# Later head groups' weights asked for by ScalarE's DMA queue, and reordered by GpSimd one unit sooner, in an attention kernel with projections

## The chip, the cores and the metric

The kernel runs on one core of one Trainium2 chip. The metric is the device time of one execution in microseconds (us); a kernel is run several times, and its median is quoted with the lowest and highest run. A run also has a span, the time from the first to the last instruction in its trace.

## The reference

Eight batches of 112 query rows, 32 heads of size 192, 512 cached keys and values for each head. All tensors are bf16.

```python
B, Sq, D = 8, 112, 640
H, Sk, Dh = 32, 512, 192
q = (x @ wq).reshape(B, Sq, H, Dh).transpose(0, 2, 1, 3)
scores = einsum("bhqd,bhkd->bhqk", q, k_cache) * Dh ** -0.5
p = softmax(scores)
o = einsum("bhqk,bhkd->bhqd", p, v_cache)
return o.transpose(0, 2, 1, 3).reshape(B, Sq, H * Dh) @ wo
```

Nearly all bytes are K and V, 50 MB each. The two weight matrices have 7.9 MB each and are read once.

## The kernel before

The work is cut into 64 units of four heads and one batch (group `g` = heads 4g to 4g+3, eight batches in a group). In unit `u` TensorE makes the scores S(u), transposes an earlier output, makes the values PV(u-1), and fills the rest with query matmuls of a later group and output matmuls of an earlier one. ScalarE does the exponentials, VectorE transposes K, GpSimd copies three quarters of V into a denser layout ("middle copy", `vm`) and reorders the columns of the query weights (`wqr` to `wqs`). SyncE asks for all data through one DMA queue, in a list that is fixed when the program is built.

```python
def load_wq(g, dc):                       # group g, one of five 128-row blocks: 192 KB
    src = wq[128 * dc:128 * (dc + 1), 4 * DH * g:4 * DH * (g + 1)]
    ...
    add(wqr[:, dc, :], src, mWQ[dc], 16 * g, [(gW, DC * (g - 2) + dc + 1)])

def load_wo(g, k):                        # two requests of 160 KB, even and odd rows
    r0 = 4 * DH * g + 256 * k
    src = wo[r0:r0 + 256].rearrange("(p e) d -> p e d", e=2)
    for e in range(2):
        add(wos[:, g % 2, 2 * k + e, :], src[:, e], mWO[g % 2][k], 32 * (g // 2 + 1), [(pO, 2 * MT * (g - 1))])

for u in range(4, NU + 1):                # SyncE's list
    if u < NU: load_k(u)
    if u - 1 >= 3: load_v(u - 1)
    for g in range(2, NG):
        d = u - max(4, 8 * (g - 1) - 6)
        if 0 <= d < DC: load_wq(g, d)
    for g in range(1, NG):
        d = u - wo_round[g]
        if 0 <= d < 3: load_wo(g, d)
```

GpSimd's loop; the reorder of a block stands five units ahead of its group, at the start of the unit:

```python
at.setdefault(8 * (g - 1) - 5 + dc if g >= 2 else -1, []).append((g, dc))
...
for u in range(NU):
    for it in at.get(u, []):
        reorder(*it)
    W(gp, vRC, u + 1)
    ...                                   # three small range checks of the softmax sums
    if u + NM < NU:
        middle(u + NM)
```

TensorE's score block: 96 small matmuls on 32 rows each (`32*128` in the traces), each with its own weight load (6,144 of both in 64 units).

```python
def do_S(u):
    ...                                   # waits for kt, qT and for the exponentials of unit u-1
    for t in range(4):
        ...
        for c in range(6):
            for a in range(4):
                p = slice(32 * a, 32 * a + 32)
                mm = pe.matmul(ps[:, a, SQ * t:SQ * (t + 1)], kt[u % NT][p, t, c // 2, :, c % 2],
                               qT[g % 2][p, c, SQ * b:SQ * (b + 1)], start=(c == 0), stop=(c == 5))
```

## Time and profile before

| | before |
|---|---|
| time, median of the 3 runs at hand | 392.45 us (391.37 to 392.5) |
| profiled span | 389.5 us |
| TensorE busy | 384.3 us |
| share of the one data queue | 91.4% of the DMA engines' time |

TensorE is busy nearly all the time and carries the chain of waits; the prediction below shows those lines and reads them. Two further views of the kernel before matter for the end of the story. The prediction has the figures of the second, but not the first. The first is from the table of DMA queues (packets, MB, share of the 16 engines):

```profile
q8 instruction: 68, 1.11, 1.2%
```

This queue carries no data of the kernel. It brings the program: 68 packets and 1.11 MB, which is 16,384 bytes each. From the waits of SyncE (us in total, times, longest):

```profile
SPq L1334 <- DVE kt L1131: 34.8, 72, 1.6
SPq L1334 <- PE ps L992: 31.6, 25, 2.9
```

SyncE waits for 66 us until K buffers (freed by VectorE) and V buffers (freed by TensorE) are empty. It has time to spare once the early stage is over.

### The profile page before, as it was taken

How to read it: one execution, taken by the hardware profiler on the slowest of the kernel's cores; microseconds unless marked ns; L12 is line 12 of the kernel's file. 1: busy time of each engine (PE TensorE's matmuls, PEld its weight loads, DVE VectorE, ACT ScalarE, POOL GpSimd, SP SyncE). 2: the span in 40 equal slices, each digit the busy share in tenths (PEclk: the TensorE clock that was granted, in tenths of full speed). 3: DMA queues.
4: the chain of work that ended last, by engine and by line, in shares of the span. 5: the costliest groups of instructions: out<-in, count | busy, mean ns of one | idle time of the engine just before them, and what ended most of it. 6: DMA issues, size and time to landing. Idle time of an engine off the chain costs nothing.

```text
span 389.5 us, 19832 instructions
## 1 busy us (share of the span) xinstructions
PE 384.3 (99%) x8833; PEld 244.2 (63%) x8286; DVE 283.9 (73%) x506; ACT 249.8 (64%) x550; POOL 153.3 (39%) x352
## 2 busy tenths in 40 slices
PE   8999989999999999999999999999999999999997
PEld 4555665656666656756666575666656566676664
DVE  1665786676786888877677687777768777788934
ACT  3767764767657766666765866676585666656662
POOL 5442544343443353333453245324533322333231
PEclk9999999999999999999999999999999999999999
DMA  8999999999998999999999999799999989889712
GB/s 271 375 369 343 334 319 347 352 332 341 335 356 289 346 337 345 342 310 320 321 319 351 320 299 310 252 312 361 322 318 340 323 282 291 277 267 325 259 40 71
DMA packets 88584, 120.00 MB, mean 308 GB/s; under 512 B 9776, under 2 KB 88496, under 8 KB 88496
## 3 DMA queue, kind: packets, MB, share of 16 engines
q1 hardware_dynamic: 88496, 118.72, 91.4%
q8 instruction: 68, 1.11, 1.2%
q14 instruction: 20, 0.16, 0.1%
HBM read 117.54 MB, written 1.15 MB: 305 GB/s over the span
## 4 chain that ended last, share of the span: by engine, by line
PE 97%; issue 1%; POOL 1%; DVE 1%; DMA 0%; ACT 0%; SPq 0%
PE ps L953 22%; PE ps L878 22%; PE ps L992 22%; PE ps L974 21%; PE ps L1003 6%; PE ps L912 2%; PE ps L897 1%; PE ps L874 1%; DMA vs<-in_v_cache_dram 0%; POOL vm L1234 0%; PE ps L917 0%; POOL wqs L1227 0%; DVE kt L1131 0%; DVE acc L1151 0%; ACT oT L1089 0%
## 5 line engine op out<-in xcount | busy, mean ns | idle before, releaser
L1131 DVE STREAM_TRANSPOSE kt<-kr 128x384 int32<-128x384 int32 x256 | 195.0, 868 | 12.9 <-DMA kr<-in_k_cache_dram 11.6
L1072 ACT ACTIVATE pT<-ps 128x448 bf16<-128x448 f32 x256 | 131.3, 560 | 88.6 <-PE ps L974 87.1
L974 PEld LDWEIGHTS ps<-qT,kt 32*128 32x128 bf16 x6144 | 77.2, 93 | 30.1 <-issue 22.0
L953 PE MATMUL ps<-wos,oT 128*128 128x320 bf16 (+2 forms) x342 | 93.0, 299 | 0.0
L992 PE MATMUL ps<-vm,pT 128*128 128x193 bf16 x768 | 91.3, 247 | 0.8 <-ACT oT L1089 0.8
L878 PE MATMUL ps<-wos,oT 128*128 128x320 bf16 x330 | 91.2, 299 | 0.0
L974 PE MATMUL ps<-qT,kt 32*128 32x112 bf16 x6144 | 87.7, 208 | 0.4 <-DVE kt L1131 0.3
L1251 POOL TENSOR_SCALAR bad<-rinv 112x4 f32<-112x4 f32 x64 | 14.7, 229 | 183.7 <-DVE rinv L1137 183.5
L1234 POOL COPY vm<-vs 128x1152 int32<-128x1152 int32 x64 | 73.5, 1149 | 27.3 <-issue 20.7
L992 PEld LDWEIGHTS ps<-vm,pT 128*128 128x128 bf16 x768 | 68.5, 97 | 20.3 <-ACT oT L1089 9.6
L953 PE MATMUL ps<-xT,wqs 128*128 128x448 bf16 x210 | 74.0, 352 | 0.7 <-POOL wqs L1227 0.7
L878 PE MATMUL ps<-xT,wqs 128*128 128x448 bf16 x210 | 73.9, 352 | 0.0
L1079 ACT ACTIVATE os<-ps,rinv 112x192 bf16<-112x192 f32 x128 | 48.1, 440 | 25.3 <-DVE rinv L1137 25.3
L992 PE MATMUL ps<-vs,pT 128*128 128x193 bf16 x256 | 62.6, 245 | 0.0
L953 PEld LDWEIGHTS ps<-wos,oT 128*128 128x128 bf16 x342 | 33.2, 97 | 43.9 <-issue 37.2
L1056 ACT ACTIVATE qT<-ps 128x448 bf16<-128x448 f32 x96 | 47.8, 554 | 16.0 <-PE ps L953 11.2
L1154 DVE TENSOR_TENSOR acc<-ps,acc 128x320 f32<-128x320 f32 x84 | 37.4, 486 | 21.2 <-PE ps L953 21.0
L1089 ACT ACTIVATE oT<-ps 128x672 bf16<-128x672 bf16 x64 | 46.4, 725 | 1.3 <-PE ps L1003 1.3
L1137 DVE RECIPROCAL rinv<-ps 112x4 f32<-112x4 f32 x64 | 11.1, 173 | 45.3 <-PE ps L992 45.3
L953 PEld LDWEIGHTS ps<-xT,wqs 128*128 128x128 bf16 x210 | 20.3, 97 | 33.2 <-issue 26.6
L1140 DVE TENSOR_TENSOR os<-ps,rinv 112x384 bf16<-112x384 f32 x64 | 35.7, 558 | 7.0
L1227 POOL COPY wqs<-wqr 128x384 bf16<-128x384 bf16 x70 | 33.4, 509 | 4.9 <-DMA wqr<-in_wq_dram 4.9
(44 smaller groups left out, 155.9 us busy)
## 6 DMA issues: line engine op xcount, KB each, us to landing
kr<-in_k_cache_dram SPq DMA_DIRECT2D x256, 192.0 KB, 4.0
vs<-in_v_cache_dram SPq DMA_DIRECT2D x256, 192.0 KB, 4.0
wos<-in_wo_dram SPq DMA_DIRECT2D x48, 160.0 KB, 4.1
wqr<-in_wq_dram SPq DMA_DIRECT2D x35, 192.0 KB, 5.2
wqs<-in_wq_dram SPq DMA_DIRECT2D x5, 192.0 KB, 4.1
out_dram<-xs SPq DMA_DIRECT2D x6, 160.0 KB, 2.1
xs<-in_x_dram SPq DMA_DIRECT2D x2, 320.0 KB, 3.2
xs<-in_x_dram SPq DMA_DIRECT2D x1, 480.0 KB, 5.3
```

Of the source, the lines that this page charges most:

```text
L878: return pe.add_instruction(mybir.InstMatmult(name=nc.get_next_instruction_name(), engine=mybir.EngineType.PE, ins=[pe.lower_ap_or_imm(rhs ...
L953: mm = (pe.matmul if h == hs[0] and f == 0 else held)(ps[:, bank_of(pair, h), cs], w, rhs[h][:, cs], q == 0, q == n - 1 and f == cuts - 1)
L974: mm = pe.matmul(ps[:, a, SQ * t:SQ * (t + 1)], kt[u % NT][p, t, c // 2, :, c % 2], qT[g % 2][p, c, SQ * b:SQ * (b + 1)], start=(c == 0), ...
L992: mm = pe.matmul(pv[:, k, e, 0:DH + 1], pT[u % 2][:, a, t, :], src[:, a, v0:v0 + DH + 1], start=(t == 0), stop=(t == 3), skip_group_check= ...
L1056: act.activation(qT[g % 2][:, c, HQ * h:HQ * (h + 1)], ps[:, bank_of_Q0(n) if g == 0 else 6 + h, 0:HQ], ACTF.Copy).then_inc(aQ, 1)
L1072: act.activation(pT[u % 2][:, a, :, 0:SQ], ps[:, a, 0:4 * SQ].rearrange("p (t q) -> p t q", t=4), ACTF.Exp, scale=scale).then_inc(aEX, 1)
L1079: ins = act.activation(os_[u % 2][:, DH * (2 + e):DH * (3 + e)], pv_of(u)[0:SQ, 1, e, 0:DH], ACTF.Copy, scale=rinv[:, u % 4, 2 + e:3 + e])
L1089: act.activation(oT[:, :, SQ * b:SQ * (b + 1)].rearrange("p (k c) q -> p k c q", k=2), src.rearrange("p k (c q) -> p k c q", c=3), ACTF.Co ...
L1131: dve.transpose(dst, src).then_inc(vKT, 1)
L1140: dve.tensor_tensor(os_[u % 2][:, 0:2 * DH].rearrange("p (e d) -> p e d", e=2), pv[0:SQ, 0, :, 0:DH], rinv[:, u % 4, 0:2][:, :, None].broa ...
L1154: ins = dve.tensor_tensor(ob[:, m, cs] if g == NG - 1 else acc[:, m, cs], src, acc[:, m, cs], op=ALU.add)
L1234: gp.tensor_copy(vm[u % NM][:].rearrange("p a (t w) -> p a t w", w=RW)[:, :, :, 0:DH].bitcast(I32), vs[u % NV][:, :, 32:32 + 3 * DH].rearr ...
```

## The change

SyncE hands 72 weight requests to ScalarE (30 of `wq` for groups 2 to 7, 42 of `wo` for groups 1 to 7), so that K and V no longer stand behind them. They also stand earlier, three or four rounds by the loops' indices. GpSimd reorders one unit sooner, and no longer at the head of the unit but after the range checks and ahead of the middle copy.

```diff
+        def weight_loads(i):
+            got = []
+            for g in range(2, NG):
+                d = i - max(1, 8 * (g - 1) - 10)
+                if 0 <= d < DC:
+                    got.append((wqr[:, d, :], wq[128 * d:128 * (d + 1), 4 * DH * g:4 * DH * (g + 1)], mWQ[d],
+                                gW, DC * (g - 2) + d + 1))
+            for g in range(1, NG):
+                k = i - (wo_round[g] - 4)
+                if 0 <= k < 3:
                     ...                              # the two requests of load_wo
+            return got
@@ on_scalar, end of a unit @@
                 evac_pair(i, 1)
+                for dst, src, s, ws, wv in weight_loads(i):
+                    W(act, ws, wv)
+                    act.dma_start(dst, src).then_inc(s, 16)
@@ on_gpsimd @@
-                    at.setdefault(8 * (g - 1) - 5 + dc if g >= 2 else -1, []).append((g, dc))
+                    at.setdefault(8 * (g - 1) - 6 + dc if g >= 2 else -1, []).append((g, dc))
             for u in range(NU):
-                for it in at.get(u, []):
-                    reorder(*it)
                 W(gp, vRC, u + 1)
                 ...
+                for it in at.get(u, []):
+                    reorder(*it)
                 if u + NM < NU:
                     middle(u + NM)
@@ on_sync @@
-                for g in range(2, NG):  ...  load_wq(g, d)
-                for g in range(1, NG):  ...  load_wo(g, d)
```

## The prediction

> **What bounds the kernel now.** I read the page first: engine shares, then the chain of work that ended last, then the waits of TensorE.

> ```profile
> PE 384.3 (99%) x8833; PEld 244.2 (63%) x8286; DVE 283.9 (73%) x506; ACT 249.8 (64%) x550; POOL 153.3 (39%) x352
> ...
> q1 hardware_dynamic: 88496, 118.72, 91.4%
> ...
> PE 97%; issue 1%; POOL 1%; DVE 1%; DMA 0%; ACT 0%; SPq 0%
> ```

> The reader should see two limits close together. TensorE is busy in 384.3 of 389.5 us and carries 97% of the chain; the one DMA queue is busy 91% of the span. A busy matmul row need not mean a full one, so I checked the starts in the chain: 320-column output matmuls follow each other every 0.135 us, 448-column query matmuls every 0.19 us, 16 value matmuls take 1.35 us and 96 score matmuls 1.29 us, unit after unit. Those are the shortest spacings that the trace has for each shape, so inside a block nothing is to be gained. What remains is idle time between blocks, which the waits of TensorE and the longest pieces of the chain show:

> ```profile
> PE ps L992 <- ACT oT L1089: 0.8, 1, 0.8
> PE ps L953 <- POOL wqs L1227: 0.7, 1, 0.7
> PE ps L974 <- DVE kt L1131: 0.3, 1, 0.3
> ```

> After the start-up I find by spacing only about 2.6 us of lost TensorE time in the whole run: 1.0 at 57.4 us (values wait for ScalarE's oT copy), 0.86 at 65.95 us (the first query matmul of group 2 waits for GpSimd's reordered weights), and four score blocks with 0.08 to 0.17 us each. Only the 0.86 belongs to the change. It is a chain, read from the timeline of GpSimd:

> ```profile
> 60.11 0.20 POOL L1254 TENSOR_TENSOR cnt<-cnt,bad 112x8 f32<-112x8 f32 x1
> 63.85 1.15 POOL L1234 COPY vm<-vs 128x1152 int32<-128x1152 int32 x1 [3.53 <-issue]
> 64.94 0.96 POOL L1227 COPY wqs<-wqr 128x384 bf16<-128x384 bf16 x2
> ```

> GpSimd was free at 60.3 us, but the middle copy of unit 8 stood first in its order and waited 3.5 us for V of unit 8 (it landed at 63.74). The last reorder of group 2 came behind it, and ended at 65.9, just when TensorE wanted it.

> Last, the early stage. SyncE issues nearly back to back until about 60 us, and the stretches show a full DMA:

> ```profile
> 20.00:40.00 20.00, 20.00 (x499) 11.99 (x473) 12.76 (x21) 14.05 (x32) 6.49 (x13) 1.00 1.04 357
> 40.00:60.00 20.00, 18.89 (x431) 12.68 (x402) 15.65 (x29) 13.65 (x30) 10.59 (x23) 1.00 0.99 324
> ...
> 240.00:380.00 140.00, 140.00 (x3372) 91.14 (x3162) 105.90 (x190) 91.17 (x203) 51.48 (x114) 1.00 0.87 284
> ```

> The last two columns are the DMA share and GB/s. Up to about 80 us K and V land just in time: the V landing starts the middle copy of units 2 to 11. Later both land 3 us or more before their readers.

> [...]

> **The change part by part.**

> (a) SyncE loses 30 query and 42 output weight requests, 72 x 0.475 us (their pitch in the trace) = 34 us of issue. After 60 us SyncE waits for DVE (34.8 us) and for TensorE (31.6 us) anyway, so that is worth nothing later. Early, the issue was already slowed by a full DMA (single issues of 1.2 to 1.6 us in place of 0.43), so little there either. Gain: about 0.

> (b) ScalarE gains 72 x 0.475 = 34 us. They stand at the end of a unit, where ScalarE waits for the next scores (87.1 us over 64 units, mean 1.36). I set requests against the idle time before, unit by unit. One request needs 0.475 and the least idle time is 0.49; two need 0.95 against 1.07 or more, but 0.80 and 0.85 in two late units. Three need 1.42, in units 3, 4, 5, 30, 38 and 39, where the idle time is 0.49, 1.07, 1.85, 1.09, 1.09 and 1.85. The excess is 0.93+0.36+0.34+0.34+0.25 = 2.2 us in all. Of that the oT copy can pass on perhaps a third, as it has about 0.1 us of room before the value matmuls where a half pair stands between, but about 0.8 after a full pair: cost 0.7 us. If the sequencer runs ahead, nothing: the requests go out while ScalarE still computes. I take 0.2.

> (c) Reorder sooner and ahead of the middle copy: it now starts at about 60.3 and ends at 61.3 (2 x 0.48), 4.6 us ahead of need. The 0.86 goes. In the other 29 units the middle copy starts up to 0.96 us later: it ends about 3.2 us after the value block, and the fourth exponential wants it after about 3.9 at least; where V is late the reorder fits into the wait. Cost 0. Gain 0.86.

> (d) Weights asked for sooner. From the trace, old requests for wq of group 2 went out at 31.1, 35.4, 40.5, 46.5 and 53.5 us, for wo of group 1 at 47.9, 54.0 and 59.6. New ones, at ScalarE's unit ends: wq at 27, 33, 39.5, 44.5, 49.5; wo at 40, 45, 50; and wq of group 3 from 55.6 in place of 65.2. At 45 to 50 us that is 0.85 MB ahead of the old order, at 57 us about 0.5, at 63 about 0.4. At 350 GB/s, K and V are late by 2.4, 1.5 and 1.1 us. Room of V before TensorE must wait (exponential 4 to the next scores): unit 4 1.6 us, unit 5 2.3, unit 6 2.5, unit 7 1.3, unit 8 1.4. So about 0.2 us is lost. [...] Such losses don't add up unit by unit: each stall gives the DMA the same time to catch up. I take 0.6.

> Sum: -0.86 + 0.2 + 0.6 = about -0.1 us. From the median before, 392.45, which is at the upper edge of its three runs (mean 392.1), I say 391.9.

> **The rivals.**
> - Gain through a freed SyncE: K and V no longer queue behind weights, the early stage runs smoother, and the other early stalls (1.0 + 0.5) shrink too. For it: 20 to 60 us of nearly gapless issue. Against: the DMA share of 1.0 there, and the 1.0 us at 57.4 has an empty slot ahead of it and a chain of exponential and oT copy that no load touches. It would give 389.8 to 390.8.
> - Early V starved: the wait for weights is replaced by one for V, and so for the fourth exponential. For it: V's room of 1.3 to 2.5 us in units 4 to 8[...]. Against: all of these bytes are needed anyway and the lead is made once. It gives 392.5 to 394.
> - ScalarE as a new bound: a request that takes 1.0 us or more[...] would exceed the idle time in some 30 units, passing on 0.2 to 0.5 us each: 6 to 15 us, 398 to 407. For it: 1.2 to 1.6 us issues of SyncE. Against: the waits on semaphores are met long before (five units for the reorder), the ScalarE queue is nearly empty of requests[...].

> **Range and chances.** The middle cases span -1.5 to +1.5 us about 392, and runs before differ by 1.1 us, which gives 389.8 to 394.2. To be 2% faster, 7.8 us would have to go where only 2.6 us are lost: 0.01. Only the third rival makes it 2% slower: 0.04. Within 2%: 0.95.

> **What would show it.** (a) A second hardware queue with some 13 MB (30 x 197 KB + 42 x 164 KB); SyncE issues 531 loads and waits more. (b) ScalarE busy as before, and its wait for scores little changed; requests from its sequencer of about 0.45 us, before the unit's end if it runs ahead. (c) TensorE's wait for wqs gone, reorders ending before the middle copy of the same unit. (d) V of units 4 to 8 landing 1 to 4 us later against TensorE, waits of ScalarE for vm above the 1.5 us of before, score blocks waiting for pT before 65 us. Wrong would be: any ScalarE request above 1 us past 80 us with a value block behind it, or a span off by more than 3 us.

## The result, and the profile after

| | before | changed |
|---|---|---|
| time, median of 6 runs each | 391.91 us (390.65 to 392.92) | 397.76 us (395.76 to 400.23) |
| profiled span | 389.5 us | 396.8 us |
| ratio of fast runs | | 1.0155, 95% interval 1.0113 to 1.0197 |

A ratio is the mean time of one kernel's fast runs over that of the other's of the same rounds, so it is not quite the ratio of the medians. The change is within 2%, as predicted, but the time lies 3.6 us above the predicted range. The profiled pair lies a little further apart (7.3 us of span) than the medians of the six runs (5.9 us). Where did 7.3 us of span come from?

The page of the changed kernel first: engine shares, queues, the head of the chain of waits, and the weight requests (KB each, median us to landing).

```profile
PE 386.1 (97%) x8833; PEld 244.8 (62%) x8286; DVE 284.1 (72%) x506; ACT 249.8 (63%) x550; POOL 153.5 (39%) x352
...
q1 hardware_dynamic: 78128, 105.94, 79.4%
q10 hardware_dynamic: 10368, 12.78, 9.8%
q8 instruction: 68, 1.11, 1.1%
...
PE 97%; issue 2%; DVE 0%; ACT 0%
...
wos<-in_wo_dram ACTq DMA_DIRECT2D x42, 160.0 KB, 4.7
wqr<-in_wq_dram ACTq DMA_DIRECT2D x30, 192.0 KB, 5.1
```

The second data queue is there with the expected 12.78 MB. No engine has more work: ScalarE has the same 249.8 us. TensorE's share fell from 99 to 97%, and in the chain "issue" rose from 1 to 2%: time in which the engine waited for nothing that the profile shows. The waits of TensorE say the same (us in total, times, longest):

```profile
PE ps L990 <- issue: 4.3, 8, 1.2
PE ps L969 <- issue: 1.9, 1, 1.9
...
PE ps L1008 <- ACT oT L1105: 0.8, 1, 0.8
PE ps L990 <- DVE kt L1150: 0.3, 1, 0.3
```

The wait for `wqs` has gone, as predicted. In its place are nine stops that name nobody, in score blocks (L990) and query or output matmuls (L969). Two of them in TensorE's timeline (start, length, what, in brackets the idle time before):

```profile
55.13 0.87 PE L990 MATMUL ps<-qT,kt 32*128 32x112 bf16 x56 [0.26 <-DVE kt L1150]
57.17 0.67 PE L990 MATMUL ps<-qT,kt 32*128 32x112 bf16 x40 [1.18 <-issue]
...
158.58 0.31 PE L969 MATMUL ps<-wos,oT 128*128 128x320 bf16 x1 [1.88 <-issue]
```

A score block has 96 matmuls and its only waits stand at its head. Here it breaks after 56. Nothing in the program is waited for between matmul 56 and 57, and no operand is late there that the program waits for. The same view of the kernel before, one block later:

```profile
60.51 1.36 PE L974 MATMUL ps<-qT,kt 32*128 32x112 bf16 x96
```

There the block is whole. The longest pieces of the chain of the changed kernel show that its breaks in this stage come at a regular distance:

```profile
49.49 0.80 PE ps L990 x55
50.29 0.49 issue
50.79 0.70 PE ps L990 x41
...
55.13 0.87 PE ps L990 x56
56.00 1.18 issue
57.17 0.71 PE ps L990 x40
...
62.24 0.80 PE ps L990 x56
63.04 0.50 issue
63.55 0.67 PE ps L990 x40
```

| from 12 us on | before | changed |
|---|---|---|
| lost at page ends | 0.72 us in 4 stops | 8.93 us in 15 stops |
| lost elsewhere | 1.03 us (0.86 of it the wait for `wqs`) | 0.17 us |
| page ends passed under 1.6 us after the fetch | 4 of 66 | 23 of 66 |
| TensorE past the last page end, to the start of a fetch, mean | 1.94 us | 2.42 us |

The changed kernel loses 8.93 + 0.17 = 9.10 us, the kernel before 0.72 + 1.03 = 1.75, and the difference of 7.3 us is the whole difference of the spans. Both kernels also have the 1.0 us at 57 us for ScalarE's `oT` copy.

The last two rows show what a stop waits for. Four fetches from the records of that queue, in us:

```
kernel    TensorE passed     fetch              TensorE passes    from fetch's end
          the last page end                     this page end     to the page end
before    50.47              52.19 to 53.07     55.48             2.41
before    55.48              57.80 to 58.68     61.17             2.49
changed   50.79              54.65 to 55.74     57.17             1.43, stopped
changed   57.17              61.01 to 62.07     63.55             1.48, stopped
```

Each of 66 fetches pairs with one page end, in order. In both kernels the fetch of a page begins at the earliest 0.9 us before TensorE's first matmul past the previous page end, and usually after it; it takes about 1.0 us (median 1.01 and 0.99); and no page end is passed sooner than 1.2 us after the packet's end. A page of TensorE's program lasts 390 / 66 = 5.9 us. Before, that leaves 5.9 - 1.9 (to the start) - 1.0 (the fetch) = 3.0 us, and the stops ended 1.2 to 1.6 us after a packet. From these means I estimate that a fetch that starts 2 us later leaves 1.0 us, too little, so that TensorE stands still. In the changed kernel fetches of the same size start later (the limits of 60 KB and 2.5 us below were chosen after the fact). Of its 66, 42 had over 60 KB of the second queue's data start in the 2.5 us before them: these began 2.84 us after the page end and 20 came too late (under 1.6 us). The other 24 began after 1.68 us, and 3 came too late. At least 8.8 of the 8.9 us are lost at page ends whose fetch had data of the second queue just ahead.

The remaining parts went nearly as the prediction said, or better. Reorder and middle copy of GpSimd:

```profile
61.53 0.20 POOL L1271 TENSOR_TENSOR cnt<-cnt,bad 112x8 f32<-112x8 f32 x1
61.79 0.96 POOL L1246 COPY wqs<-wqr 128x384 bf16<-128x384 bf16 x2
62.69 1.16 POOL L1253 COPY vm<-vs 128x1152 int32<-128x1152 int32 x1
```

The reorder no longer stands behind a middle copy that waits for V. ScalarE's requests, with its own work beside them:

```profile
43.17 0.42 ACT L1095 ACTIVATE os<-ps,rinv 112x192 bf16<-112x192 f32 x1 [1.01 <-DVE rinv L1156]
43.18 0.34 ACTq L1136 DMA_DIRECT2D wqr<-in_wq_dram  x1
43.49 0.41 ACT L1095 ACTIVATE os<-ps,rinv 112x192 bf16<-112x192 f32 x1
43.55 0.94 ACTq L1136 DMA_DIRECT2D wos<-in_wo_dram  x2
44.98 0.54 ACT L1088 ACTIVATE pT<-ps 128x448 bf16<-128x448 f32 x1 [1.08 <-PE ps L990]
```

The first request went out at 43.18 us, ahead of the activation at 43.49 that stands before it in the program. Three requests end at 44.49, before the scores that ScalarE waits for anyway. They cost nothing here. And the early stage (columns: stretch, its length, busy time and count of TensorE, weight loads, VectorE, ScalarE and GpSimd, then clock, DMA share and GB/s):

```profile
20.00:40.00 20.00, 20.00 (x502) 12.17 (x469) 13.31 (x21) 14.42 (x32) 7.15 (x15) 1.00 1.07 371
40.00:60.00 20.00, 17.22 (x411) 11.60 (x387) 14.34 (x26) 12.19 (x28) 9.39 (x19) 1.00 1.07 372
```

From 40 to 60 us the DMA moves 372 GB/s where it moved 324. K and V came hardly later for the weights put ahead: V of unit 6 landed at 51.19 us (50.48 before), V of unit 7 already at 56.75 (57.27 before). But TensorE, busy 18.89 us of this stretch before, has 17.22 now. The data that came sooner bought nothing. SyncE simply waits more for empty buffers:

```profile
SPq L1345 <- PE ps L1008: 68.8, 38, 4.6
SPq L1345 <- DVE kt L1150: 55.9, 89, 4.4
```

### The profile page after: what moved, and what is told of

Read it like the earlier page. It is cut to its first block, busy times and chain, and to the rows that moved or that the text cites. A ratio compares the mean times of both kernels' runs of the same rounds, so it can differ in the third digit from the quotient of the medians.

```text
span 396.8 us, 19856 instructions
## 1 busy us (share of the span) xinstructions
PE 386.1 (97%) x8833; PEld 244.8 (62%) x8286; DVE 284.1 (72%) x506; ACT 249.8 (63%) x550; POOL 153.5 (39%) x352
## 2 busy tenths in 40 slices
DMA packets 88585, 120.01 MB, mean 302 GB/s; under 512 B 9776, under 2 KB 88496, under 8 KB 88496
## 3 DMA queue, kind: packets, MB, share of 16 engines
q10 hardware_dynamic: 10368, 12.78, 9.8%
HBM read 117.54 MB, written 1.15 MB: 299 GB/s over the span
## 4 chain that ended last, share of the span: by engine, by line
PE 97%; issue 2%; DVE 0%; ACT 0%
PE ps L969 22%; PE ps L894 22%; PE ps L1008 21%; PE ps L990 21%; PE ps L1019 6%; PE ps L928 2%; PE ps L913 1%; PE ps L890 1%; PE ps L933 0%; DVE kt L1150 0%; ACT oT L1105 0%; DVE acc L1170 0%; PE ps L1025 0%; ACT pT L1088 0%; DVE xs L1173 0%
## 5 line engine op out<-in xcount | busy, mean ns | idle before, releaser
L990 PEld LDWEIGHTS ps<-qT,kt 32*128 32x128 bf16 x6144 | 77.6, 93 | 35.7 <-issue 27.7
L969 PE MATMUL ps<-wos,oT 128*128 128x320 bf16 (+2 forms) x342 | 93.1, 299 | 1.9 <-issue 1.9
L990 PE MATMUL ps<-qT,kt 32*128 32x112 bf16 x6144 | 89.3, 208 | 4.7 <-issue 4.3
L969 PE MATMUL ps<-xT,wqs 128*128 128x448 bf16 x210 | 74.0, 352 | 0.0
L969 PEld LDWEIGHTS ps<-wos,oT 128*128 128x128 bf16 x342 | 33.2, 97 | 46.0 <-issue 39.3
L969 PEld LDWEIGHTS ps<-xT,wqs 128*128 128x128 bf16 x210 | 20.3, 97 | 32.4 <-issue 26.8
```

Source lines behind the costliest of these rows:

```text
L969: mm = (pe.matmul if h == hs[0] and f == 0 else held)(ps[:, bank_of(pair, h), cs], w, rhs[h][:, cs], q == 0, q == n - 1 and f == cuts - 1)
```

## The experiments

The theory to test: (F) TensorE's program comes late because a second queue of data is active, so that the fetches of instructions begin later. Rivals: (R) GpSimd's new order does it; (A) ScalarE as issuer does it; (C) the weights are asked for too early and crowd out K, V or the fetches, on whatever queue; (N) the number of small requests does it. All time ratios are against the kernel before in the same rounds.

### 1. The reorder alone

The weights go back to SyncE's list; only GpSimd's two edits stay.

```diff
@@ against the changed kernel @@
-        def weight_loads(i): ...
-                for dst, src, s, ws, wv in weight_loads(i):
-                    W(act, ws, wv)
-                    act.dma_start(dst, src).then_inc(s, 16)
@@ on_sync @@
+                for g in range(2, NG):
+                    d = u - max(4, 8 * (g - 1) - 6)
+                    if 0 <= d < DC:
+                        load_wq(g, d)
+                for g in range(1, NG):  ...  load_wo(g, d)
```

> Only the reorder moves (one unit sooner, ahead of the middle copy); all weights stay on SyncE's queue. Theory A (the second hardware queue makes TensorE's instruction fetches late, which stops TensorE at every 256th instruction): no such stop above 0.3 us, the 0.86 us wait for wqs gone, ratio 0.996 to 1.000 (390.4 to 392 us). Rival B (the reorder ahead of the middle copy holds up the exponentials): ratio 1.008 or more. Rival C (weights asked for sooner crowd out K and V): ratio as under A, as nothing is asked for sooner.

Measured: 392.70 us median (391.53 to 395.36), ratio 0.9995 (0.9957 to 1.0033). The waits of TensorE in the profiled run, which was the slowest of the six:

```profile
PE ps L974 <- issue: 1.1, 2, 0.7
...
PE ps L992 <- ACT oT L1089: 0.8, 1, 0.8
...
PE ps L953 <- issue: 0.3, 1, 0.3
```

The wait for `wqs` is gone and three stops at page ends have 1.91 us (0.53, 0.94 and 0.44), so I missed with "no stop above 0.3": one queue alone can now and then be late too. GpSimd shows why the order matters, and not only the unit:

```profile
61.80 0.95 POOL L1227 COPY wqs<-wqr 128x384 bf16<-128x384 bf16 x2
64.09 1.15 POOL L1234 COPY vm<-vs 128x1152 int32<-128x1152 int32 x1 [1.34 <-DMA vs<-in_v_cache_dram]
```

The middle copy still waits for V, but with the reorder already done. The gain of 0.86 us does not come out of the scatter of the time. (R) falls.

### 2. The second queue alone

The reverse: GpSimd's loop as before, weights on ScalarE's queue.

```diff
@@ against the changed kernel, on_gpsimd @@
-                    at.setdefault(8 * (g - 1) - 6 + dc if g >= 2 else -1, []).append((g, dc))
+                    at.setdefault(8 * (g - 1) - 5 + dc if g >= 2 else -1, []).append((g, dc))
             for u in range(NU):
+                for it in at.get(u, []):
+                    reorder(*it)
                 W(gp, vRC, u + 1)
```

> Only the requests move to ScalarE's queue at their new times; the reorder stands where it stood before. Theory A: the loss stays whole, ratio 1.013 to 1.022, with 10 or more stops of TensorE at instructions that are 193 modulo 256 in its order and 6 us or more lost in them. Rival B: ratio below 1.004. Rival C: loss stays, but as waits on K or V before 80 us, not at these instructions.

Measured: 398.79 us (395.22 to 400.52), ratio 1.0137 (1.0088 to 1.0186), and 10.70 us lost in 15 stops at page ends.

```profile
PE ps L990 <- issue: 5.7, 9, 1.5
PE ps L969 <- issue: 1.9, 2, 1.6
```

The whole loss is in the queue.

### 3 and 4. Only `wq`, or only `wo`, on ScalarE's queue

Number 3 keeps the 30 `wq` requests on ScalarE (5.9 MB), number 4 the 42 of `wo` (6.9 MB); the other half goes back to SyncE's list at its old places.

```diff
@@ number 3, weight_loads @@
-            for g in range(1, NG):
-                k = i - (wo_round[g] - 4)
-                ...
@@ number 3, on_sync @@
+                for g in range(1, NG):  ...  load_wo(g, d)
@@ number 4, weight_loads @@
-            for g in range(2, NG):
-                d = i - max(1, 8 * (g - 1) - 10)
-                ...
@@ number 4, on_sync @@
+                for g in range(2, NG):  ...  load_wq(g, d)
```

> Only the 30 query weight requests (5.9 of 12.8 MB) go by ScalarE's queue; the 42 output weight requests stay on SyncE's; reorder as in the change. Theory A: a part of the loss by the bytes on the second queue, ratio 1.003 to 1.010, stops only near the times of query weight requests. Rival C (time of asking): most of the loss from the early query weights, so nearly the whole 1.015.

> Only the 42 output weight requests (6.9 of 12.8 MB, in pairs one after the other) go by ScalarE's queue; query weights stay on SyncE's; reorder as in the change. Theory A: the larger part of the loss, ratio 1.006 to 1.014, stops near the output weight requests (130 to 160, 240 to 260, 300, 360 us). Rival B: below 1.004.

Measured: `wq` alone 396.74 us (394.35 to 398.76), ratio 1.0092 (1.0051 to 1.0133); `wo` alone 400.79 us (398.35 to 401.17), ratio 1.0191 (1.0150 to 1.0233), above what I expected. The lost time at page ends is 6.24 us in 12 stops and 6.58 us in 13, so either half does it, and together they cost less than the sum. In both kernels the time is 4.2 to 4.9 us above the span in all runs but one (2.3 us), where it is 1.7 to 1.8 elsewhere. By the medians of the spans they are 1.8 us (392.0) and 6.0 us (396.2) longer than before (390.2); some 3 us of each lies outside the traced execution, and I have no cause for it. The profiled run of number 3 is the slowest of its six (span 394.2), so its 6.24 us are probably more than a usual run of it lost. Nor did its stops keep to the times of the requests, as expected: 0.88 us were lost at 14.5 us, before the first of them, and 0.68 us in three stops after the last.

Number 4 also shows what followed a stop. Its timeline:

```profile
57.30 0.67 PE L985 MATMUL ps<-qT,kt 32*128 32x112 bf16 x40 [1.37 <-issue]
...
59.22 0.43 PE L1003 MATMUL ps<-vm,pT 128*128 128x193 bf16 x3 [0.84 <-ACT oT L1100]
...
60.03 0.69 PE L1003 MATMUL ps<-vm,pT 128*128 128x193 bf16 x3
```

After these two pauses of 1.37 and 0.84 us three value matmuls take 0.69 us in place of 0.43: from 59.7 us TensorE runs at half its clock for 3.41 us (mean granted clock of this run 0.996), which costs 1.6 us more. That the pauses bring it on was not shown. Such a stretch takes 0.4% off the mean clock of a run (my estimate, half of 3.41 us in 396). Three of the six runs of the changed kernel have a mean clock of 0.996, so such a stretch probably occurred in them too; the profiled run had none before its end.

### 5. The same kernel with the program shifted

If stops belong to pages of the program, 64 tiny matmuls put ahead of everything must shift where in the computation they fall, but not their number in the stream.

```diff
@@ on_tensor, before the first query matmuls @@
                 (held if j else pe.matmul)(ps[:, 7, 0:128], wt[:], wt[:], True, True)
+            for j in range(64):
+                held(ps[:, 7, 0:2], wt[:], wt[:, 0:2], True, True)
```

> The changed kernel with 64 more tiny matmuls (2 columns) for TensorE ahead of all others: the same work, 64 instructions later in TensorE's stream. Theory A (late fetches of 256 instructions each): the stops stay at instructions that are 193 modulo 256 of the stream, so they fall on other matmuls of the program than before, 64 instructions earlier in it; 4 to 12 us lost in them in all. Rival (stops tied to a place in the program, a buffer or a wait): they stay at the same matmuls, so at 1 modulo 256.

Measured (one run): 397.37 us, span 395.6. Ten stops of 5.68 us, at 2241, 2497, 4033, 4545, 6593, 8641, 8897, 11201, 12225 and 13249: all still leave 193 when divided by 256. The 0.17 us wait for `kt`, which belongs to the computation, moved from number 2129 to 2193, by exactly 64.

```profile
PE ps L990 <- issue: 3.6, 6, 1.0
```

So the stops hold to the pages of the instruction stream, not to a place in the computation. Together with the times of the fetches that settles what TensorE waits for.

### 6. GpSimd as the issuer

The same requests at GpSimd, after the range checks of the unit, so that ScalarE issues none. GpSimd's requests go through a queue of another kind (`software_dynamic` in the page below, where ScalarE's was `hardware_dynamic`), and have their own semaphores.

```diff
@@ on_scalar @@
-                for dst, src, s, ws, wv in weight_loads(i):
-                    W(act, ws, wv)
-                    act.dma_start(dst, src).then_inc(s, 16)
@@ on_gpsimd @@
                 gp.wait_ge(gC, u + 2)
+                for dst, src, s, ws, wv in weight_loads(u + 1):
+                    W(gp, ws, wv)
+                    gp.dma_start(dst, src).then_inc(s, 16)
                 for it in at.get(u, []):
```

> The weights of later groups are requested by GpSimd (another queue again, its own semaphores), not by ScalarE, at the end of GpSimd's checks of a unit. Theory A (any second data queue beside SyncE's makes the fetches late): stops at 193 modulo 256 again, 4 us or more lost in them, ratio 1.008 to 1.03 (GpSimd's own time for the requests may add). Rival D (it is ScalarE as the issuer that costs): stops vanish, ratio below 1.005 unless GpSimd becomes late.

Measured: 395.81 us (395.52 to 397.32), ratio 1.0121 (1.0086 to 1.0156), 5.71 us in 10 stops at page ends. The queue, and the waits of TensorE:

```profile
q0 software_dynamic: 3936, 12.78, 9.5%
```

```profile
PE ps L992 <- issue: 2.6, 5, 0.8
...
PE ps L971 <- issue: 0.8, 2, 0.6
...
PE ps L1021 <- issue: 0.4, 1, 0.4
```

The same bytes, another issuer, packets over twice as large (3,936 for 12.78 MB), and the same kind of loss. Of its 24 fetches with this queue's data ahead, 11 were late, of the other 42 only 3. (A) falls: it is a second queue of data that matters, not which engine fills it.

### 7. Weights sooner, but on one queue

Rival (C): the reorder in its new place, no second queue, and the weights moved forward in SyncE's list to about the time at which ScalarE asked for them.

```diff
@@ on_sync, against number 1 @@
-                    d = u - max(4, 8 * (g - 1) - 6)
-                    if 0 <= d < DC:
-                        load_wq(g, d)
+                    for d in range(DC):
+                        if u == (4 + d // 2 if g == 2 else 8 * (g - 1) - 8 + d):
+                            load_wq(g, d)
-                    d = u - wo_round[g]
+                    d = u - (5 if g == 1 else wo_round[g])
```

> One queue (SyncE) as before, reorder as in the change, but the weights stand earlier in SyncE's list: query weights of group 2 in steps 4 to 6 in place of 4 to 8, those of later groups two steps sooner, output weights of group 1 in steps 5 to 7 in place of 7 to 9. Theory A: ratio 0.997 to 1.004, under 2.5 us lost at 193 modulo 256. Rival C (earlier requests crowd out K and V): ratio 1.006 or more, with waits on K or V before 80 us.

Measured: fast runs of 391.21, 392.56, 394.69 and 394.78 us, ratio 1.0062 (1.0024 to 1.0100). The profile is of a fifth run, 400.0 us in the slow state, so its length says nothing, but what waited for what does. The chain:

```profile
49.55 6.27 DMA vs<-in_v_cache_dram
55.87 1.16 POOL vm L1234
57.11 0.55 ACT pT L1072
57.80 2.43 PE ps L974 x96
```

V of unit 6 landed at 55.82 us (50.48 before), the middle copy had to wait, then the exponential, then TensorE. This is the crowding of V that the prediction feared under (d), seen on one queue. With two it did not appear. So (C) is a second way to lose time, and not what the changed kernel's trace shows. Two reservations: the crowding is shown in a slow run alone, so what the fast runs lost is open, and that trace also lost 3.29 us in six stops at page ends, more than the 2.5 us that I expected on one queue. A second queue with the requests at their old times was not tried. But in the changed kernel 5.0 of the 8.9 us were lost after 150 us, where its requests go out between 2 us sooner and 5 us later than before, so there earliness is no likely cause.

### 8. Fewer requests on one queue

A try for a winner, and half of a test of (N): both halves of a `wo` block as one request with rows of 2,560 bytes, on SyncE, with the reorder in its new place.

```diff
-                for e in range(2):
-                    add(wos[:, g % 2, 2 * k + e, :], src[:, e], mWO[g % 2][k], 32 * (g // 2 + 1), [(pO, ...)])
+                add(wos[:, g % 2, 2 * k:2 * k + 2, :], src, mWO[g % 2][k], 16 * (g // 2 + 1), [(pO, ...)])
```

> A try at beating both: one queue, reorder as in the change, and each pair of output weight requests made one request with rows of 2560 bytes (24 requests in place of 48). Theory A: nothing new on a second queue, so no added stops; TensorE is at its spacing, so at best the 0.86 us and part of the early stops go: ratio 0.993 to 1.000.

Measured: 394.00 us (392.94 to 397.42), ratio 1.0082 (1.0043 to 1.0120): a miss, not a winner. The profiled span is 388.9 us, with 1.21 us in five stops, but the spans of the six runs reach from 388.9 to 395.7 (median 391.7), and the time lies 1.6 to 4.2 us beyond the span. One trace of the shortest run does not explain this scatter.

### 9. More data on the second queue

If the second queue does it, twice the bytes on it should cost more: the changed kernel, with one of the four V requests of each unit moved to ScalarE.

```diff
@@ weight_loads @@
+            if 4 <= i + 3 < NU:
+                g, b = divmod(i + 3, B)
+                got.append((vs[(i + 3) % NV][:, 3, 32:32 + 4 * DH], v_cache[b, 4 * g + 3].rearrange("(m t) d -> m (t d)", t=4),
+                            mV[(i + 3) % NV], pPV, i))
@@ load_v @@
-                for a in range(4):
+                for a in range(4 if u < 4 else 3):
```

> More of the suspected cause: the changed kernel with one of the four V requests of every unit from unit 4 on also on ScalarE's queue (60 x 197 KB, so 24.6 MB on the second queue in place of 12.8), at the same point of the computation; total bytes the same. Theory A: more fetches late, 12 to 25 us lost at instructions 193 modulo 256, ratio 1.025 to 1.05. Rival (the loss comes from weights alone, or from when they are asked for): ratio near the changed kernel's own 1.0155.

Measured: 405.45 us over four runs (399.49 to 407.96, the upper two slow), ratio of the fast runs 1.0369 (1.0299 to 1.0440). It is the slowest of all. Its profile, of the fastest run:

```profile
q10 hardware_dynamic: 19008, 24.58, 18.3%
```

```profile
PE ps L994 <- issue: 6.6, 8, 1.8
```

There 9.37 us are lost in 13 stops, hardly more than in the changed kernel and below what I expected. 20 of 66 page ends come under 1.6 us after their fetch. So twice the bytes did make it slower, but the trace at hand is of the one run that was least slow, and what the longer runs lost is not shown.

### 10. `wo` alone on ScalarE, in half the requests

Rival (N) once more: number 4 with its 42 requests merged into 21.

```diff
@@ against number 4, weight_loads @@
-                    for e in range(2):
-                        got.append((wos[:, g % 2, 2 * k + e, :], src[:, e], mWO[g % 2][k], pO, 2 * MT * (g - 1)))
+                    got.append((wos[:, g % 2, 2 * k:2 * k + 2, :], src, mWO[g % 2][k], pO, 2 * MT * (g - 1)))
```

> The kernel with only the output weights on ScalarE's queue (its ratio was 1.019), each pair made one request with rows of 2560 bytes: 21 requests in place of 42, the same bytes. If the number of requests counts: ratio near 1.009. If the bytes on the second queue count: 1.014 to 1.022.

Measured: 401.19 us (397.93 to 402.87), ratio 1.0237 (1.0150 to 1.0324), a little above both expectations; 5.63 us in 13 stops, and again about 3 us at half pace after the stop of 1.65 us at 58.4 (mean granted clock 0.996). That is number 4 again (1.0191). Half the requests and half the packets, the same loss: (N) falls.

### 11. The changed kernel again

> The changed kernel once more, on the same chip as the two above, as their measure and for a second trace: ratio 1.012 to 1.020; theory A: again 6 us or more lost at 193 modulo 256, though at partly other times than in the first trace[...].

Measured on another occasion: 399.37 us (398.84 to 400.42), ratio 1.0188 (1.0128 to 1.0249), 8.92 us in 16 stops, and a stretch at half pace from 60 us (mean granted clock 0.996). Nine of the 15 page ends at which the first trace stopped stop again (1985, 2241, 6081, 6337, 6593, 8641, 11201, 15809, 16065), but with other lengths: number 6593 lost 2.05 us there and 0.95 here. Others come or go: 4033 (101.1 us) is new with 1.27 us, and 13249 with 0.98 us is gone. So the places repeat in part and the lengths do not; why they differ was not shown. That the two sums are so close I take for chance.

All traces in one table, by what the second queue carries (the profiled run of each; number 7's is slow and left out: 7 page ends, 3.29 us):

| kernel | MB on second queue | page ends under 1.6 us after the fetch | us lost there | ratio of times |
|---|---|---|---|---|
| before | 0 | 4 of 66 | 0.72 | 1 |
| 1, reorder alone | 0 | 7 | 1.91 | 0.9995 |
| 8, fewer requests | 0 | 5 | 1.21 | 1.0082 |
| 3, `wq` | 5.9 | 17 | 6.24 | 1.0092 |
| 4, `wo` | 6.9 | 17 | 6.58 | 1.0191 |
| 10, `wo` merged | 6.9 | 17 | 5.63 | 1.0237 |
| 6, by GpSimd | 12.8 | 14 | 5.71 | 1.0121 |
| 5, shifted | 12.8 | 18 | 5.68 | one run |
| changed | 12.8 | 23 | 8.93 | 1.0155 |
| 11, changed again | 12.8 | 23 | 8.92 | 1.0188 |
| 2, queue alone | 12.8 | 21 | 10.70 | 1.0137 |
| 9, and a quarter of V | 24.6 | 20 | 9.37 | 1.0369 |

(In number 8, the time lost at page ends does not account for the ratio; see there.) With one data queue it is 4 to 7 page ends of 66 and in the fast state under 2 us, with two it is 14 to 23 and 5.6 us or more. The loss does not grow in step with the bytes on the second queue.

One rival was not on my list: that it is the amount of data, on whatever queue, that makes a fetch late. The traces can be asked. On one queue (before, 1 and 8 together) fetches do start later after more data: 1.63 us past the page end where 600 to 750 KB had started in the 2.5 us before, 2.47 us with 850 to 1000 KB. But at equal amounts the second queue adds to it: with 750 to 850 KB it was 2.04 us on one queue (73 fetches) and 2.64 us (106 fetches) where over 60 KB of them were the second queue's. So both count.

None of these kernels beats the one before; number 1 is its equal.

## Why the prediction was wrong

The class was right (within 2%) and the time was wrong: 391.9 predicted, at most 394.2, 397.76 measured. That the class held is luck: the loss came from a cost that the prediction did not have, and happened to stay under 2%. Step by step:

- **What bounds the kernel.** Right that TensorE has only about 2.6 us to gain (the parts listed add up to 2.4). The step that failed lies here: after "inside a block nothing is to be gained" the prediction looked only at idle time between blocks, as waits for engines and data, and so gave the supply of TensorE's program no cost. The runs showed 8.93 us lost for it, at places where the program waits for nobody. That supply was in the same page, a queue with 68 packets of program, and the trace before already had its four stops: one of 0.35 us in the start-up, and three of the "four score blocks with 0.08 to 0.17 us each" (0.17, 0.12 and 0.08). I took them for noise. Numbering them would have given 193 modulo 256, and the room would have followed from the trace before: 5.9 us a page, less 1.9, less 1.0, less the 1.2 to 1.6 after which the stops ended.
- **(a) SyncE's requests.** "Gain: about 0" was right for the time, and its reason was wrong. A DMA share of 1.0 was read as a full DMA, but the share reached 1.07 with two queues, and the rate from 40 to 60 us rose from 324 to 372 GB/s. One queue with fewer requests (number 8) reached 361 there, so it need not be the second queue that did it. The faster data only made SyncE wait more for empty buffers (124.7 us in place of 66.4), as TensorE does not read sooner.
- **(b) ScalarE's requests.** Right. They lie beside ScalarE's last activations and before the next scores, and its busy time did not change; the rival with requests of over 1.0 us fell (single requests up to 1.35 us occur, none over 0.81 us past 80 us, with no value block held up by them). The measured time lies next to that rival's 398 to 407 us, but not for its reason. The sequencer ran ahead by an instruction or two (the request at 43.18 us, ahead of the activation at 43.49).
- **(c) The reorder.** Right. The 0.86 us went in the changed kernel and in number 1.
- **(d) V crowded by early weights.** The cost of 0.6 us, an estimate of mine above the 0.2 from the room of V, was wrong: 0 in the changed kernel, where the rate was higher (372 against 324 GB/s) and V at most 0.7 us later in these units. On one queue (number 7) the mechanism does appear, with V of unit 6 over 5 us late.
- **The sum.** -0.86 for (c) came true. The missing term is +8.2 us (8.93 - 0.72, of the profiled pair) for late pages of TensorE's program. It belongs to no rival of mine: the three that I listed are about SyncE, V and ScalarE. (The stated range of 2.2 us to each side is not the sum of the figures that it is said to come from, 1.5 and 1.1.) "Early, the issue was already slowed by a full DMA" looked only at bandwidth, when the question that decided was what a second queue does to the delay of a third, tiny one (fetches began 1.94 us past the page end before, 2.42 changed).

What is shown: the stops that name nobody are at page ends and nowhere else (number 5 ties them to the stream), each ends 1.2 to 1.6 us after a page's packet, fetches start later when the second queue has just been active, at equal amounts of data too, and the loss comes with a second queue whoever fills it (2, 3, 4, 6, 10) and not with the other edits (1, 8). What is not shown: why the fetch begins later. How the DMA engines choose between queues was not seen. Open are also why `wo` on the second queue costs more than `wq` (6.0 against 1.8 us of span for 6.9 and 5.9 MB), the 3 us or so outside the span in numbers 3, 4, 10 and part of 8, what number 9's longer runs lost, and why number 7's and 8's fast runs are slower than the kernel before.

## What to carry to other kernels

On an engine that is busy all the time with thousands of small instructions, count the supply of its program as an operand: take the time of a page, less the start of its fetch and the fetch itself, and see how much room is left (here 5.9 - 1.9 - 1.0 = 3.0 us, of which a stop used 1.2 to 1.6) before adding a queue of data. A transfer rate can rise with a second queue and the kernel still get slower (here from 324 to 372 GB/s between 40 and 60 us, and from 391.91 to 397.76 us). A stop that names nobody inside a block is a reason to number the instructions and look for a period.
